# Zero-padded attention products: a second copy of the queries, last values laid out per head, 8 exp buffers for 12

## The chip, the cores and the metric

The kernel runs on one core of a Trainium2 chip. The metric is the device time of one launch in microseconds (us); lower is better. The engines are PE (matrix products; PEld is its loading of weights, that is of the operand that stays in the array), DVE and ACT (elementwise work), POOL (slower elementwise work) and SP, which here only issues DMAs.

## What is computed

```python
# attention: q, k, v are (4, 8, 576, 64)
q_rot, k_rot = (rotate(q), rotate(k))
scores = scale * np.matmul(q_rot, k_rot.transpose(0, 1, 3, 2))
scores = scores - np.max(scores, axis=-1, keepdims=True)
attn = np.exp(scores)
attn = attn / (np.sum(attn, axis=-1, keepdims=True) + 1e-09)
return np.matmul(attn, v)
# then, on the (2304, 512) result: a gated layer, (sigmoid(x Wg) * (x Wv)) Wo with d_ff 1536,
# and a layer of 8 experts, each token through one of them
```

The gated layer and the experts are not touched by the change.

## The kernel before

Attention works on 16 pairs of heads, one after the other. Products are made of two parts, a high and a low one, so that precision is kept: every matrix is split in a rounded high part and the rest.

A pair has nine score tiles (`scores`, line 164). Tile t = 2j + x below 8 is 128 queries of head x against the 576 keys, in two halves of 288 columns. It has two products. The first has 128 rows: high and low part of the queries stand one above the other in `q2`, and the high part of the keys stands twice in `kh`. The second has the high queries against the low keys `kl`; as a head has 64 dimensions, it has 64 rows, those of the head (`q2[r, x, qs]`, `kl[r]`). Tile 8 takes the last 64 queries of both heads; its third product uses `qd`, which holds the queries on a diagonal with zeros beside them, and so has 128 rows already.

DVE scales a tile out of PSUM into a buffer `e` (ring of E_BUFS), with the row's extreme (line 190); ACT takes the exponential (line 202). PE transposes it (line 234; the last 64 keys apart, line 249), ACT copies the high part out (`pth`, line 264; `p5h` for the last keys), DVE the low part (`ptl`, `p5l`, line 268). A value product (`value`, line 270) exists four times per pair, for head x and the query ranges 0 to 255 and 256 to 575: ten products into one PSUM buffer `pv`, eight of them with 128 rows for the first 512 keys, and two with 64 rows, `vv[r, 8]` against `p5h` and `p5l`, for the last 64 keys. ACT copies half of `pv`, DVE adds the other half to it.

The operands of a pair are prepared while earlier pairs run (`plan_prep`, from pair 2 on): a load from HBM, the rotation on POOL, the split, and then twelve copies by DMA from `hq` and `hk` into `q2`, `qd` and `kh` (line 448). These operands exist twice, for even and odd pairs: a pair's copies may begin when the score tiles of the pair two before are done, and its score tiles wait for all of them. The pairs 0 and 1 are prepared by the engines instead (`plan_direct`).

The order on each engine is set by a list scheduler (`Plan`): costs in us and priorities by tile decide which operation comes next; rings of buffers bound how far it goes ahead. SP, too, takes its DMAs in that order, each when the one before it has been issued.

Of the kernel before, what the change touches and what calls it, by code (L numbers as in the profile page):

```python
# [7 lines left out]
F32 = mybir.dt.float32  # L8
# [8 lines left out]
NP = H // 2  # L17
# [5 lines left out]
E_BUFS = 12  # L23
PT_BUFS = 3
ST_BUFS = 3
# [6 lines left out]
class Plan:  # L32
    """Orders instructions of several in-order engines: a list schedule over their dependences.
    Costs and latencies (us) only steer the order; the waits themselves are Tile's.
    A ring is a set of rotating buffers: an op that takes the next one has to stand behind the
    op that reads the old contents last."""
# [70 lines left out]
class Attention:  # L107
    def __init__(self, tc, pool, xpool, psum_s, psum_t, psum_v, qk, v, rope, ident, xt, rows):
        self.tc, self.nc = tc, tc.nc
        self.pool, self.xpool, self.ps_s, self.ps_t, self.ps_v = pool, xpool, psum_s, psum_t, psum_v  # L110
        self.qk, self.v, self.xt, self.rows = qk, v, xt, rows
        nc = self.nc
        self.rope = rope
        self.ident = ident
        t = lambda shape, dt, name: pool.tile(shape, dt, name=name, tag=name, bufs=1)
        self.pth = t([128, KC, 2 * S], F32R, "pth")
        self.ptl = t([128, KC, 2 * S], F32R, "ptl")
        self.p5h = t([128, S], F32R, "p5h")
        self.p5l = t([128, S], F32R, "p5l")
        self.vv = [t([128, 9, 2, D], F32R, f"vv_{i}") for i in range(2)]  # L120
        self.kl = [t([128, S], F32R, f"kl_{i}") for i in range(2)]
        self.qd = [t([128, 128], F32R, f"qd_{i}") for i in range(2)]
        sa = xpool.tile([128, 7 * S], F32R, name="sa", tag="sa", bufs=1)
        self.raw = f32(sa[:, 0:4 * S]).rearrange("p (a s) -> p a s", a=4)
        self.hqk = sa[:, 4 * S:7 * S].rearrange("p (a s) -> p a s", a=3)
        self.hq, self.hk = self.hqk[:, 0:2], self.hqk[:, 2]
        sb = xpool.tile([128, 4 * S + 4 * 640], F32R, name="sb", tag="sb", bufs=1)
        kh = sb[:, 0:4 * S].rearrange("p (i x s) -> p i x s", i=2, x=2)
        q2 = sb[:, 4 * S:].rearrange("p (i x s) -> p i x s", i=2, x=2)
        self.q2, self.kh = ([a[:, i] for i in range(2)] for a in (q2, kh))  # L130
        self.xv = t([128, 320], F32, "xv")
        self.vraw = t([128, 9, D], F32, "vraw")
        for i in range(2):
            nc.vector.memset(f32(self.q2[i][:, 0, S:640]), 0.0)
            nc.vector.memset(f32(self.q2[i][:, 1, 512:S]), 0.0)
            nc.vector.memset(f32(self.qd[i]), 0.0)
        self.e, self.s, self.pt, self.pv = {}, {}, {}, {}
        self.stat, self.ready, self.rt, self.rr = {}, {}, {}, {}
        self.plan = Plan(dict(s=2, e=E_BUFS, pt=PT_BUFS, pv=1))
        self.ids = {}  # L140

# [21 lines left out]
    def scores(self, T):  # L163
        """tile t of a pair: t = 2 j + x is queries 128 j.. of head x; t = 8 the last 64 of both heads"""
# [8 lines left out]
        else:  # L173
# [3 lines left out]
            mm = [(q2[:, x, qs], kh[:, x]), (q2[r, x, qs], kl[r])]  # L177
# [16 lines left out]
    def column(self, T):  # L194
        """statistics of a tile; columns of a head stand together"""
# [21 lines left out]
    def recip_rows(self, p, x, part):  # L217
        """the reciprocal sums of head x (its first 512 queries, or the rest) into each of its 64 partitions"""
# [25 lines left out]
    def transpose5(self, p, part):  # L244
        """the last 64 keys: head 1 in partitions 64.. (after 64 other keys), then head 0 in 0.."""
# [24 lines left out]
    def value(self, p, x, u):  # L270
# [4 lines left out]
        r = slice(64 * x, 64 * x + 64)  # L275
# [4 lines left out]
        mm += [(vv[r, 8], h[r, c0:c0 + w]) for h in (self.p5h, self.p5l)]  # L280
# [34 lines left out]
    def frees(self, last, first):  # L315
        """op last reads the buffer that op first took"""
# [39 lines left out]
    def plan_direct(self, p, pr):  # L356
        """the first pairs: rotation shared by two engines, operands doubled by the engines"""
# [6 lines left out]
        for half in (1, 0):  # L364
            j = 2 * half
            for n, c in enumerate(self.cuts(p, half)):
# [21 lines left out]
                for x in range(2):  # L388
                    last = min(c.stop, 512) if x else c.stop
                    cuts = [(c.start, last, 0)] + ([(512, S, 64)] if last < c.stop else [])  # L390
                    for a, b, d in cuts:
# [9 lines left out]
                        if a < 512:  # L401
                            for t in range(c.start // 128, 4):
                                need[x, t] = keys
# [8 lines left out]
    def plan_prep(self, p):  # L412
# [27 lines left out]
        for x in range(2):  # L440
            r = slice(64 * x, 64 * x + 64)
            cp.append((0, self.qd[i][r, r], self.hq[r, 0, 512:S]))
        for x in range(2):
# [23 lines left out]
    def plan_tile(self, T):  # L467
# [3 lines left out]
        self.op(("s", T), "PE", (0.74 if t == 8 else 0.5) * (1 if T > 4 else 2), lambda: self.scores(T), ready, T + o["s"], "s")  # L471
# [55 lines left out]
    def plan_value(self, p, x, u):  # L527
# [4 lines left out]
        self.op(("value", p, x, u), "PE", 10 * w / 2350, lambda: self.value(p, x, u),  # L532
# [34 lines left out]
def pack(q, k, v):  # L567
# [10 lines left out]
    vp = np.concatenate([vm, vp[:, :, :, 512:].reshape(B, NP, 128, 1, D)], axis=3)  # L578
# [22 lines left out]
class Gated:  # L601
    """x -> (sigmoid(x Wg) * (x Wv)) Wo, weights given as 64-bit words."""
# [16 lines left out]
    def convert(self, f, m, dma):  # L619
        """float64 words -> float32 (truncated) -> two float32r parts; returns (engine, cost, closure) in order."""  # L620
# [55 lines left out]
    def early_x(self, u):  # L676
        """parts of a unit's x in the memory that the last pair's rotation leaves"""
# [6 lines left out]
    def gate_val(self, f, u, keep=None):  # L684
        """keep: a free [128, 2, U] area for the result, instead of a pair of rotating tiles"""
# [12 lines left out]
    def gv_mm(self, f, m, p, xh, xl, chunks, part=None):  # L698
        """part 0: the products with the high part of x; 1: those with the low part; None: both, chunk by chunk"""
# [16 lines left out]
    def early(self, at, npairs):  # L716
        """the first units' part of the first matrix pair, in the engines' free time at the end of the attention;
        its results wait in the memory of later matrices"""
# [69 lines left out]
    def convert_group(self, grp):  # L788
        """closures; each matrix's load stands one matrix ahead of its arithmetic"""
# [8 lines left out]
    def opening(self):  # L798
        """the rest of the first group and the second; leaves the second's last unit to its out product"""
# [135 lines left out]
    def last(self, prev, r, experts):  # L935
        """The last group: all of its g first, with the router's logits from the y so far and from g;
        then its part of y, while the routing is worked out."""
# [37 lines left out]
        def before(u, prio):  # L975
            """the group before: its part of y"""
# [11 lines left out]
        def fold(prio):  # L988
            """the router's weights behind the last out matrices"""
# [125 lines left out]
def bc(ap, axis, n):  # L1115
    """insert a broadcast axis of size n"""
# [4 lines left out]
class Router:  # L1121
# [59 lines left out]
    def fold(self, k, c, parts, ps_pool):  # L1181
        """the router's weights behind an out matrix: wc = wo wg, split in two parts"""
# [46 lines left out]
    def route(self, plan, start, ps_pool, area):  # L1229
        """adds the routing of all tokens to the plan"""  # L1230
# [6 lines left out]
        def do(eng, cost, deps, fn, name=None):  # L1237
            """deps None: behind the one before"""
# [137 lines left out]
class Experts:  # L1376
# [10 lines left out]
    def keep_warm(self, n):  # L1387
        """products that nobody reads: the tensor engine's clock halves when it waits long"""
# [5 lines left out]
    def place(self):  # L1394
        """claims the memory in the order in which the part before frees it: what is written first last"""
# [11 lines left out]
    def load(self, s, k, dma=None):  # L1407
        """start loading part k of the weights of the expert of slot s"""
# [93 lines left out]
    def half1(self, s, h, x):  # L1502
        """first layer of half a slot: tokens in the output's partitions"""
# [27 lines left out]
    def half2(self, s, h, hx):  # L1531
        """second layer of half a slot"""
# [135 lines left out]
```

## Time and profile before

| | us |
|---|---|
| median of 3 runs | 1082.15 (1081.64 to 1085.84) |
| span of the profiled execution | 1086.7 |

The profiled execution shows its span alone, from its first to its last instruction; it is 4.5 us over the median of the runs, and over the slowest of them too. Attention takes about the first 365 us of the span; what follows is the gated layer and the experts. A busy PE in a profile is not PE at its peak: matmuls are pipelined, and what a matmul costs in a row of them is the distance between the starts of two, not the length shown for one.

### The profile page before, as it was taken

What the parts mean: (1) busy time and instruction counts of PE and PEld (TensorE: products, weight loads), DVE (VectorE), ACT (ScalarE), POOL (GpSimd) and SP (SyncE); (2) the same over time, 40 slices, a digit from 0 to 9 for tenths busy, and PEclk for the clock granted to TensorE, in tenths of its full rate; (3) what the DMA queues carried; (4) which work ended last, traced back from release to release, by engine and by line L of the source; (5) the groups of instructions that cost most, each with busy time, mean ns of one, the idle gap of its engine ahead of it and who ended that gap; (6) DMA issues with size and microseconds to landing.
All of it is one profiled execution on the core that took longest, in us unless ns stands there. A gap on an engine that the chain in (4) does not pass through costs nothing.

```text
span 1086.7 us, 16486 instructions
## 1 busy us (share of the span) xinstructions
PE 1044.1 (96%) x6035; PEld 916.1 (84%) x6035; DVE 663.1 (61%) x1175; ACT 531.9 (49%) x1051; POOL 380.2 (35%) x288
## 2 busy tenths in 40 slices
PE   4999999999999999999999999999998899999996
PEld 3778787877778899999999999999876699999995
DVE  6888887877777673653554444543247665555561
ACT  4877777877677742222222222223331555455552
POOL 4678657668430242322331322221142111121111
PEclk9999999999899999999999999999997999999998
DMA  5456565556421130210110111100015877776750
GB/s 183 133 160 174 140 179 145 142 153 157 121 69 58 42 117 21 60 40 20 59 59 20 59 40 40 39 1 1 1 49 183 284 238 223 243 224 221 222 177 23
DMA packets 71737, 122.78 MB, mean 113 GB/s; under 512 B 13967, under 2 KB 37151, under 8 KB 71648
## 3 DMA queue, kind: packets, MB, share of 16 engines
q1 hardware_dynamic: 57728, 104.07, 33.0%
q0 software_dynamic: 3040, 9.70, 2.7%
q10 hardware_dynamic: 10880, 7.87, 2.3%
q8 instruction: 50, 0.82, 0.3%
q14 instruction: 39, 0.32, 0.1%
HBM read 95.13 MB, written 9.77 MB: 97 GB/s over the span
## 4 chain that ended last, share of the span: by engine, by line
PE 72%; issue 15%; DMA 5%; DVE 4%; POOL 1%; ACT 1%; ACTq 0%; SPq 0%; POOLq 0%; DVEq 0%
PE gv L705 27%; PE yo L771 13%; PE s L180 10%; PE pv L282 10%; PE pt L234 6%; DMA out<-e_y,r_si 5%; PE pt L249 2%; POOL e_xg L1436 1%; PE s L705 1%; PE r_pl L1205 1%; PE r_pt L1169 1%; DMA rope<-in_rope 0%; POOL out L1499 0%; PE r_pl L1212 0%; DVE sb L396 0%
## 5 line engine op out<-in xcount | busy, mean ns | idle before, releaser
L714 POOL TENSOR_TENSOR gl<-sg,gh 128x384 fp32r<-128x384 f32 x60 | 64.2, 1069 | 258.6 <-ACT gh L713 258.6
L712 DVE TENSOR_TENSOR sg<-gv,sg 128x384 f32<-128x384 f32 x70 | 39.0, 557 | 141.5 <-PE gv L705 119.5
L190 DVE TENSOR_SCALAR_CACHE_REDUCE e<-s 128x576 f32<-128x576 f32 x144 | 107.1, 748 | 24.0 <-PE s L180 22.8
L202 ACT ACTIVATE e<-e,st 128x576 f32<-128x576 f32 x144 | 112.0, 780 | 5.6 <-DVE e L190 5.4
L1429 DVE TENSOR_TENSOR e_w<-wr,e_w 128x1024 fp32r<-128x1024 f32 x80 | 95.9, 1222 | 28.9 <-ACT e_w L1428 28.6
L711 ACT ACTIVATE sg<-gv 128x384 f32<-128x384 f32 x70 | 34.3, 490 | 140.4 <-PE gv L705 140.3
L268 DVE TENSOR_TENSOR ptl<-pt,pth 128x512 fp32r<-128x512 f32 x144 | 95.3, 683 | 10.6 <-ACT pth L264 9.5
L180 PE MATMUL s<-sb 128*128 128x288 f32 x320 | 81.1, 344 | 16.2 <-DVE sb L396 14.7
L264 ACT CAST pth<-pt 128x512 fp32r<-128x512 f32 x144 | 80.3, 587 | 30.2 <-PE pt L234 29.0
L1428 ACT CAST e_w<-wr 128x1024 fp32r<-128x1024 f32 x80 | 81.4, 1047 | 26.6 <-DMA x_rows<-xy 22.5
L1484 PE MATMUL e_py<-e_w,e_hh 128*128 128x512 f32 x288 | 89.7, 393 | 0.0
L159 POOL TENSOR_TENSOR sa<-sa,rope 128x1152 f32<-128x1152 f32 x28 | 74.5, 2663 | 32.2 <-DMA sa<-in_qk 27.3
L234 PE MATMUL pt<-cst,e 128*128 128x128 f32 x576 | 84.0, 285 | 1.6 <-DVE ptl L268 1.6
L1499 POOL DMA_INDIRECT out<-e_y,r_si x19 | 19.6, 1030 | 187.4 <-ACT e_y L1498 187.4
L1466 PE MATMUL e_ph<-e_xh,e_w 128*128 128x256 f32 x576 | 82.1, 286 | 0.7 <-ACT e_xh L1449 0.7
L713 ACT CAST gh<-sg 128x384 fp32r<-128x384 f32 x60 | 30.8, 514 | 101.1 <-DVE sg L712 101.0
L282 PE MATMUL pv<-pth,vv 128*128 128x256 f32 (+1 forms) x256 | 75.8, 318 | 3.6 <-DVE vv L347 2.2
L705 PE MATMUL gv<-xe,wb 128*128 128x384 f32 x384 | 78.9, 338 | 0.0
L1466 PEld LDWEIGHTS e_ph<-e_xh,e_w 128*128 128x128 f32 x576 | 75.9, 195 | 1.5 <-ACT e_xh L1449 0.9
L234 PEld LDWEIGHTS pt<-cst,e 128*128 128x128 f32 x576 | 64.7, 144 | 13.6 <-issue 8.2
L705 PE MATMUL gv<-xh,wb 128*128 128x384 f32 x288 | 74.1, 338 | 0.0
L180 PEld LDWEIGHTS s<-sb 128*128 128x128 f32 x320 | 49.3, 196 | 27.8 <-DVE sb L396 14.7
(242 smaller groups left out, 2496.1 us busy)
## 6 DMA issues: line engine op xcount, KB each, us to landing
wr<-in_w SPq DMA_DIRECT2D x74, 512.0 KB, 4.1
sa<-in_qk SPq DMA_DIRECT2D x30, 576.0 KB, 4.7
sb<-sa SPq DMA_DIRECT2D x84, 144.0 KB, 4.9
wraw<-in_wg SPq DMA_DIRECT2D x12, 512.0 KB, 3.9
wraw<-in_wv SPq DMA_DIRECT2D x12, 512.0 KB, 3.5
wraw<-in_wo SPq DMA_DIRECT2D x12, 512.0 KB, 3.6
vraw<-in_v SPq DMA_DIRECT2D x16, 288.0 KB, 5.2
x_rows<-xy ACTq DMA_DIRECT2D x18, 256.0 KB, 2.6
```

Of the source, the lines that this page charges most:

```text
L180: nc.tensor.matmul(ps[:, u, 0:SH], a, m[:, SH * u:SH * u + SH], start=n == 0, stop=n == len(mm) - 1)
L190: self.nc.vector.tensor_scalar(out=e, in0=ps[:, :, 0:SH], scalar1=-0.125, scalar2=3.0e38, op0=ALU.mult, op1=ALU.min, accum_out=st[:, 0])
L202: nc.scalar.activation(out=e, in_=e, func=AF.Exp, bias=st[:, 0], scale=-1.0, accum_out=st[:, 1])
L234: nc.tensor.transpose(pt[:, c], e[:, 128 * c:128 * c + 128], self.ident)
L268: self.nc.vector.tensor_tensor(out=lo, in0=src, in1=f32(hi), op=ALU.subtract)
L282: nc.tensor.matmul(ps[:, 0:w], a, m, start=n == 0, stop=n == len(mm) - 1)
L705: self.nc.tensor.matmul(p[:, 0:U], a[:, wc], b[:, c], start=c == 0 and n == 0, stop=c == KC - 1 and n == 2)
L771: nc.tensor.matmul(ps, a, b, start=n == 0, stop=n == 3 * len(GROUPS[grp]) - 1)
L1428: nc.scalar.copy(out=hi, in_=raw)
L1429: nc.vector.tensor_tensor(out=lo, in0=raw, in1=f32(hi), op=ALU.subtract)
L1466: nc.tensor.matmul(ps[:, k], a[:, fs], b[:, c], start=n == 0, stop=n == 3 * KC - 1)
L1484: nc.tensor.matmul(ps, a[:, f, hs], b, start=n == 0, stop=n == 23)
```

## The change

The second product of a score tile gets 128 rows in all pairs but the first. Its queries come from a new tile `qz`, which holds the high queries of head x in that head's 64 rows and zeros in the other 64, and it takes all rows of `kl`. The two products with the last 64 keys get 128 rows as well: the values of the last keys are stored once per head, with zeros in the rows of the other head. `qz` is filled by two more DMAs per pair; the loads of the values grow from 576 to 640 columns. The ring of `e` has 8 buffers for 12, that of the row statistics 2 for 3. The scheduler's costs of score tiles and value products change, so the order on the engines moves. (The diff also removes docstrings, which are left out here.)

```diff
-E_BUFS = 12
+E_BUFS = 8
 PT_BUFS = 3
-ST_BUFS = 3
+ST_BUFS = 2
...
-        self.vv = [t([128, 9, 2, D], F32R, f"vv_{i}") for i in range(2)]
+        self.vv = [t([128, 10, 2, D], F32R, f"vv_{i}") for i in range(2)]
...
+        self.qz = [t([128, 2, 512], F32R, f"qz_{i}") for i in range(2)]
...
+            for x in range(2):
+                nc.vector.memset(f32(self.qz[i][64 - 64 * x:128 - 64 * x, x]), 0.0)
...
-            mm = [(q2[:, x, qs], kh[:, x]), (q2[r, x, qs], kl[r])]
+            mm = [(q2[:, x, qs], kh[:, x]), (q2[r, x, qs], kl[r]) if p == 0 else (self.qz[i][:, x, qs], kl)]
...
-        mm += [(vv[r, 8], h[r, c0:c0 + w]) for h in (self.p5h, self.p5l)]
+        mm += [(vv[:, 8 + x], h[:, c0:c0 + w]) for h in (self.p5h, self.p5l)]
...
+                            if p > 0:
+                                self.dma(("qz", *key), 0.4, lambda x=x, i=slice(a, min(b, 512)): nc.sync.dma_start(
+                                    out=f32(self.qz[p][r[x], x, i]), in_=f32(q2[r[x], x, i])), [("qhi", *key)], pr + 1.5 + x + n)
...
             cp.append((0, self.qd[i][r, r], self.hq[r, 0, 512:S]))
+            cp.append((0, self.qz[i][r, x], self.hq[r, 0, 0:512]))
...
-        self.op(("s", T), "PE", (0.74 if t == 8 else 0.5) * (1 if T > 4 else 2), lambda: self.scores(T), ready, T + o["s"], "s")
+        self.op(("s", T), "PE", (0.81 if t == 8 else 0.54 if p else 0.92) * (1 if T > 4 else 2), lambda: self.scores(T), ready, T + o["s"], "s")
...
-        self.op(("value", p, x, u), "PE", 10 * w / 2350, lambda: self.value(p, x, u),
+        self.op(("value", p, x, u), "PE", 10 * (w / 2400 + 0.0135), lambda: self.value(p, x, u),
...
-    vp = np.concatenate([vm, vp[:, :, :, 512:].reshape(B, NP, 128, 1, D)], axis=3)
+    ve = np.zeros((B, NP, 2, 64, 2, D), v.dtype)
+    for x in range(2):
+        ve[:, :, x, :, x] = vp[:, :, x, 512:]
+    vp = np.concatenate([vm, ve.reshape(B, NP, 128, 2, D)], axis=3)
```

Two places show how instructions move. The first is PE behind tile 8 of pair 8 (`s<-kl_0,qd_0` is that tile's last product; the score tiles behind it are those of pair 9, `pt` are transposes). Before:

```order
L180 MATMUL s_2214<-kl_0_99,qd_0_101 128x288 x2
L180 MATMUL s_2225<-sb_104 128x288 x2
L180 MATMUL s_2225<-kl_1_100,sb_104 128x288 x2
L234 MATMUL pt_2234<-cst_60,e_2103 128x128 x4
L234 MATMUL pt_2242<-cst_60,e_2113 128x128 x4
L180 MATMUL s_2251<-sb_104 128x288 x2
L180 MATMUL s_2251<-kl_1_100,sb_104 128x288 x2
L234 MATMUL pt_2259<-cst_60,e_2137 128x128 x4
L180 MATMUL s_2267<-sb_104 128x288 x2
L180 MATMUL s_2267<-kl_1_100,sb_104 128x288 x2
```

Of the change:

```order
L183 MATMUL s_2251<-kl_0_99,qd_0_101 128x288 x2
L237 MATMUL pt_2262<-cst_60,e_2067 128x128 x4
L183 MATMUL s_2271<-sb_106 128x288 x2
L183 MATMUL s_2271<-kl_1_100,qz_1_104 128x288 x2
L237 MATMUL pt_2279<-cst_60,e_2145 128x128 x4
L183 MATMUL s_2288<-sb_106 128x288 x2
L183 MATMUL s_2288<-kl_1_100,qz_1_104 128x288 x2
L237 MATMUL pt_2297<-cst_60,e_2190 128x128 x4
L183 MATMUL s_2304<-sb_106 128x288 x2
L183 MATMUL s_2304<-kl_1_100,qz_1_104 128x288 x2
```

The second product of a tile reads `qz` in place of `q2` (which lies in `sb`), and one transpose stands between two score tiles. No instruction is added on PE.

The second place is SP, from the first copy of pair 9 to its last (`sa<-in_qk` are loads of later queries and keys, `vraw` one of values; `sb<-sa`, `qd` and `qz` are the copies). Before:

```order
L448 DMA sb_104<-sa_103 64x576 x2
L326 DMA sa_103<-in_qk 128x1152
L448 DMA sb_104<-sa_103 64x576 x2
L448 DMA sb_104<-sa_103 64x512
L448 DMA sb_104<-sa_103 64x64
L448 DMA sb_104<-sa_103 64x512
L448 DMA sb_104<-sa_103 64x64
L448 DMA qd_1_102<-sa_103 64x64 x2
L448 DMA sb_104<-sa_103 64x576 x2
```

Of the change:

```order
L455 DMA sb_106<-sa_105 64x576 x2
L328 DMA sa_105<-in_qk 128x1152
L455 DMA sb_106<-sa_105 64x576 x2
L455 DMA sb_106<-sa_105 64x512
L455 DMA sb_106<-sa_105 64x64
L455 DMA sb_106<-sa_105 64x512
L455 DMA sb_106<-sa_105 64x64
L455 DMA qd_1_102<-sa_105 64x64
L455 DMA qz_1_104<-sa_105 64x512
L455 DMA qd_1_102<-sa_105 64x64
L455 DMA qz_1_104<-sa_105 64x512
L338 DMA vraw_108<-in_v 128x640
L455 DMA sb_106<-sa_105 64x576 x2
```

Twelve copies and one load have become fourteen copies and two loads.

## Rows read from the trace of the kernel before

**Rows 1.** The page: span, busy time, and the chain that ended last.
```profile
span 1086.7 us, 16486 instructions
PE 1044.1 (96%) x6035; PEld 916.1 (84%) x6035; DVE 663.1 (61%) x1175; ACT 531.9 (49%) x1051; POOL 380.2 (35%) x288
...
PE 72%; issue 15%; DMA 5%; DVE 4%; POOL 1%; ACT 1%; ACTq 0%; SPq 0%; POOLq 0%; DVEq 0%
```
**Rows 2.** Busy us (instructions) per engine by stage, granted clock, DMA share, GB/s.
```profile
28.00:65.00 37.00, 33.20 (x207) 26.12 (x207) 31.21 (x66) 30.26 (x70) 26.77 (x17) 1.00 0.53 146
...
110.00:280.00 170.00, 169.43 (x1058) 135.06 (x1057) 136.41 (x310) 132.56 (x313) 114.23 (x69) 1.00 0.61 157
```
**Rows 3.** Products with `qd` (two per pair): durations, first and last start.
```profile
L180 PE MATMUL s<-kl,qd x32: 291/295/302, 30.9 to 334.3; 128*128 128x288 f32 x32
```
**Rows 4.** Who waited for whom from 100 to 350 us: total, times, longest.
```profile
POOL sa L159 <- DMA sa<-in_qk: 20.5, 11, 5.6
PEld s L180 <- issue: 20.0, 120, 0.3
POOL kl L431 <- PE s L180: 17.8, 5, 6.5
DVE e L190 <- PE s L180: 15.2, 17, 1.7
```
**Rows 5.** Timeline of PE and PEld, two score tiles, then a value product of 256 columns.
```profile
200.25 0.50 PE L180 MATMUL s<-sb 128*128 128x288 f32 x2
...
200.68 0.29 PEld L180 LDWEIGHTS s<-kl,sb 64*128 64x128 f32 x2 [0.16 <-issue]
...
202.06 0.39 PE L282 MATMUL pv<-pth,vv 128*128 128x256 f32 x1
...
202.40 0.19 PEld L282 LDWEIGHTS pv<-ptl,vv 128*128 128x128 f32 x1
...
202.52 0.28 PE L282 MATMUL pv<-ptl,vv 128*128 128x256 f32 x1
...
202.99 0.28 PE L282 MATMUL pv<-ptl,vv 128*128 128x256 f32 x1
...
203.63 0.88 PE L249 MATMUL pt<-cst,e 128*128 128x128 f32 x6
```
**Rows 6.** Timeline of PE: tile 8 of pair 9, and what follows.
```profile
213.30 0.43 PE L180 MATMUL s<-kl,qd 128*128 128x288 f32 x2
213.57 0.60 PE L234 MATMUL pt<-cst,e 128*128 128x128 f32 x4
```
**Rows 7.** Timeline of PE: a value product of 320 columns, first to last, and what follows.
```profile
277.46 0.41 PE L282 MATMUL pv<-pth,vv 128*128 128x320 f32 x1
...
278.00 0.31 PE L282 MATMUL pv<-ptl,vv 128*128 128x320 f32 x1
...
278.58 0.31 PE L282 MATMUL pv<-ptl,vv 128*128 128x320 f32 x1
...
279.30 0.87 PE L249 MATMUL pt<-cst,e 128*128 128x128 f32 x6
```
**Rows 8.** Timeline of SP: first and last copies of pair 11, then its first tile on PE.
```profile
215.75 1.12 SPq L448 DMA_DIRECT2D sb<-sa  x2
...
223.83 2.52 SPq L448 DMA_DIRECT2D sb<-sa  x4
...
233.49 0.43 PE L180 MATMUL s<-sb 128*128 128x288 f32 x2
```
**Rows 9.** Copies issued from 220 to 250 us: issue, and time to landing.
```profile
L448 SPq DMA_DIRECT2D sb<-sa x17: 461/588/2634, 219.6 to 245.9; - x17
...
DMA to landing us min/median/max: 2.5/4.1/5.3
```
**Rows 10.** Timeline of DVE: the memsets, the first load's use, two later instructions.
```profile
1.21 0.11 DVE L135 MEMSET sb<- 128x64 f32 x1
1.30 0.17 DVE L136 MEMSET qd<- 128x128 f32 x1
5.78 0.46 DVE L161 TENSOR_TENSOR sa<-sa,rope 128x288 f32<-128x288 f32 x1 [4.31 <-DMA rope<-in_rope]
...
205.20 0.73 DVE L190 TENSOR_SCALAR_CACHE_REDUCE e<-s 128x576 f32<-128x576 f32 x1
...
205.87 0.67 DVE L268 TENSOR_TENSOR ptl<-pt,pth 128x512 fp32r<-128x512 f32 x1
```
**Rows 11.** Two stretches around a wait of PE, columns as in the second group.
```profile
282.00:284.30 2.30, 0.93 (x7) 0.56 (x6) 2.24 (x3) 1.46 (x3) 2.22 (x2) 0.99 0.01 2
284.30:291.10 6.80, 6.80 (x27) 5.80 (x27) 4.01 (x9) 2.38 (x5) 1.98 (x2) 0.50 0.16 47
```

More of the change, by code (lines that the diff above doesn't have):

```diff
@@ L131, in __init__ @@
         self.xv = t([128, 320], F32, "xv")
-        self.vraw = t([128, 9, D], F32, "vraw")
+        self.vraw = t([128, 10, D], F32, "vraw")
         for i in range(2):
@@ L274, in value @@
         cs = slice(S * x + c0, S * x + c0 + w)
-        r = slice(64 * x, 64 * x + 64)
         ps = self.ps_v.tile([128, 512], F32, name="pv", tag="pv")
@@ L401, in plan_direct @@
                         if a < 512:
+                            if p > 0:
+                                self.dma(("qz", *key), 0.4, lambda x=x, i=slice(a, min(b, 512)): nc.sync.dma_start(
+                                    out=f32(self.qz[p][r[x], x, i]), in_=f32(q2[r[x], x, i])), [("qhi", *key)], pr + 1.5 + x + n)
+                                keys = keys + [("qz", *key)]
                             for t in range(c.start // 128, 4):
```

## The prediction

> **What bounds the kernel now.** First the page: PE is busy for 96% of the span and makes 72% of the chain that ended last, and a further 15% of that chain is "issue", time in which an engine waited for nothing that the profile shows [rows 1]. Next the windows by stage. From 110 to 280 us, in attention, PE is busy for 169.4 of 170 us, DVE for 136.4, ACT for 132.6, POOL for 114.2 [rows 2]. The two `qd` products, which run once per pair, go from 30.9 to 334.3 us: 303.4 over 15 pairs, so 20.2 us per pair [rows 3]. A pair thus uses 16.2 us of DVE (136.4 / 170 x 20.2), 15.8 of ACT, 13.6 of POOL, and all of PE. The waits agree: DVE waits for PE's scores, while PE's weight loads for scores wait 120 times, 20.0 us in total, for "issue" [rows 4].
>
> What that issue time is shows in the timeline. Two score tiles begin at 200.25 and are over at 202.06, where a value product begins: 0.905 us for a tile's four products of 288 columns. Between them the weight load of the 64-row product stands idle for 0.16 us and then begins together with its matmul [rows 5]. Inside the value product, with 128 rows throughout, a weight load of 0.19 us begins at 202.40, its matmul at 202.52, and the matmul before it still runs: starts are 0.12 us apart (202.52 to 202.99 is four of them) [rows 5]. So a product is cheap next to others with 128 rows, and dear where 64 rows begin, go on or end.
>
> **Prices with 128 rows throughout.** For 288 columns, the `qd` products already have 128 rows: two in 0.27 us (213.30 to 213.57), 0.135 each [rows 6]. For 256 columns 0.118 [rows 5]. For 320, four in 0.58 us (278.00 to 278.58), 0.145 each [rows 7].
>
> **What it removes on PE.** A score tile: 4 x 0.135 = 0.54 instead of 0.905, 0.365 less, eight times per pair: 2.9 us. A value product of 256 columns takes 1.57 us now (202.06 to 203.63) [rows 5], and ten at 0.118 make 1.18; one of 320 takes 1.84 (277.46 to 279.30) [rows 7], and ten at 0.145 make 1.45. That is 0.39 each, four per pair: 1.6 us. In all 4.5 us of 20.2, which leaves PE at 15.7 per pair. Pair 0 keeps its 64-row score products. Columns are not added, and the number of products is the same. That zeros cost nothing beyond the rows they fill is taken from `qd`, half of which is zeros.
>
> A rule of the Trainium skill speaks against this. Its page "TensorE: Matmul & The Clock Gate", Part 3 (Packing small matmuls), says that a weight load overlaps with running matmuls only when its row group differs, and its section "Why this matters for your kernels" says that a product with few rows takes as long as a full one, so that small ones should be kept in separate rows. By that, padding would save nothing here and the time would stay at 1082. The loads at 202.40 overlap within one row group [rows 5], so on this point the trace disagrees.
>
> **What it adds.** Two copies of 128 KB per pair on SP; a copy's issue takes 0.59 us (median) [rows 9], so 1.2 us per pair. Four memsets of 512 columns on DVE: 64 columns take 0.11 us and 128 take 0.17 [rows 10], so some 0.5 us each, 2.1 in all, beside the 4.31 us for which DVE waits for its first load [rows 10]: nothing; without that cover 2 us. Wider value tiles (640 columns for 576) on ACT or POOL: a ninth of one operation of each, under 0.2 us per pair, on engines that have room. The smaller rings: with 8 buffers DVE can take three tiles of the next pair before the last transposes of this one (line 249) have read theirs, with 12 seven. The trace shows no wait of that kind; I take zero, and half a microsecond per pair as the upper end.
>
> **What is late next.** PE at 15.7 is not alone any more: DVE needs up to 16.2 us. Instructions on DVE overlap a little (one of 0.73 us begins at 205.20, the next at 205.87) [rows 10]; with some 37 per pair (310 / 170 x 20.2) at 0.06 this makes 14 to 16.2. And there is the chain of the copies. Pair 9's last tile is done at 213.57 [rows 6]; only then may pair 11's operands be written (POOL's wait of 17.8 us for PE, at line 431, is this one [rows 4]); the first copy is issued at 215.75, the last of the last four ends its issue at 226.35, so was issued at 225.8 [rows 8], and lands 2.5 to 4.1 us later [rows 9], at 228.3 to 229.9. Pair 11 starts on PE at 233.49 [rows 8], so this chain now has 3.6 to 5.2 us to spare. With 1.2 us more it has 2.4 to 4.0 us, and a period of 20.2 can shrink by no more than that: to 16.2 to 17.8 us.
>
> So three limits lie between 15 and 18 us, where one stood alone at 20.2. The nearest rows for such a state are those from 28 to 65 us, where PE is not the only bound: PE busy for 33.2 of 37 us, 90% [rows 2]. 15.7 / 0.9 would be 17.4; the middle of the copies' limits is 17.0. I take 17.2, 3.0 us less per pair.
>
> **The sum.** The two pairs behind pair 0 are paced by their preparation (those same 37 us), and I give them 2 us together; 13 pairs at 3.0 make 39. That is 41 us. The profiled span of 1086.7 goes to 1045.7; the runs, whose median lies 4.5 us lower, go to 1041. The ends: 0 if padding saves nothing, 13 x 4.5 + 2 = 60 if PE keeps pace alone. One loss is in the 20.2 already: from 282.0 to 284.3 PE is busy for 0.93 of 2.3 us, and in the 6.8 us behind it the granted clock is 0.50, the lower of its two levels (1.2 GHz of 2.4) [rows 11], which costs 3.4 us. I count one such event in the changed kernel as well.
>
> **The rivals.**
> - PE stays the bound: copies begin earlier, DVE's overlap is full, and a pair takes 15.7 to 16.3 us. For it: DVE at 80% and POOL at 67% leave room [rows 2]. Against it: the copies' chain. Gain 13 x 4.2 + 2 = 57, time 1025; chance 0.15.
> - The other engines keep more of it: DVE and ACT in order, each behind the other, with two or three PSUM buffers between them, and PE's clock falls more often, as PE now idles in places. A pair takes 18 to 19.5 us. Gain 13 x 1.5 + 2 = 21, time 1061; chance 0.17.
> - Padding does not do what it says: a 128-row load behind a 128-row score product is as slow as now. Against it: `qd` [rows 6]. Time 1082; chance 0.03. The page of the Trainium skill named above, in the two sections named, would come out here.
> - It ends slower: the copies become the bound at more than 20.2 us per pair. The queue of SP carries them in order behind loads; one issue in [rows 9] took 2.63 us instead of 0.59. It decides when the two new copies, with what they hold up, lengthen the chain by over 5.2 us instead of 1.2. At 6.2 a pair takes 21.2 us: 13 x 1.0 = 13 us more, 1095. For it: DMA is busy for 61% already [rows 2]. Against it: the other issues are far shorter, and the median landing is 4.1 us. Chance 0.04.
>
> **How the numbers follow.** The forecast, 16.4 to 18 us per pair (1029 to 1052), has 0.61; its middle is 1041. For 8 in 10, the range takes in most of the first rival's cases and two thirds of the second's: 1020 to 1065. About 0.5% (5.4 us) is what a measurement of this kernel can tell from no change. Faster by more than that: 0.61 + 0.15 + 0.16 = 0.92. Within it: 0.01 of the second rival and most of the third, 0.04. Slower: 0.04.
>
> **What the changed profile would show.** Score products of 288 columns start 0.135 us apart, and "issue" disappears from the waits of PE's loads; if it stays there, the removal is wrong. The `qd` products come every 17.2 us. PE shows waits within attention where it had almost none, for DVE or for the copies; if for the copies mostly, the chain above is the bound; if for none, the first rival holds. The stages behind attention take as long as before; if they move by several us, the sum misses a term. The forecast fails most easily in the 17.2, which is a choice between limits and not a row.

## The result, and the profile of the changed kernel

The changed kernel takes 1059.22 us (median of 4 runs, 1056.3 to 1062.35), the kernel before 1083.88 (4 runs, 1081.64 to 1085.84): a ratio of 0.9768, with a 95% interval of 0.9741 to 0.9794. That is 24.7 us less, where 41 was forecast. The time stands where the second rival put it (1061). Both profiled executions are the longest of their four runs, 3.1 us over the median for the changed kernel and 2.0 for the kernel before. The page of the changed kernel: span, busy time, and the chain that ended last.

```profile
span 1060.5 us, 16517 instructions
PE 994.1 (94%) x6035; PEld 912.6 (86%) x6035; DVE 664.0 (63%) x1179; ACT 532.9 (50%) x1051; POOL 386.3 (36%) x288
...
PE 52%; issue 17%; DMA 12%; DVE 9%; ACT 4%; POOL 3%; SPq 2%; ACTq 0%; POOLq 0%; DVEq 0%
```

PE's share of the chain fell from 72% [rows 1] to 52%, and DMA, 5% of it before, has 12%. The windows (columns as in [rows 2]):

```profile
28.00:65.00 37.00, 33.82 (x220) 30.95 (x220) 34.95 (x74) 29.46 (x70) 28.98 (x19) 0.95 0.65 182
...
110.00:265.00 155.00, 137.16 (x1007) 128.48 (x1007) 128.09 (x293) 127.96 (x298) 109.96 (x67) 0.98 0.69 178
```

In attention PE was busy for 99.7% of the time [rows 2]; now for 137.16 of 155 us, 88%. No engine is full: DVE and ACT are busy for 83%. The `qd` products answer to [rows 3]:

```profile
L183 PE MATMUL s<-kl,qd x32: 291/295/442, 35.6 to 312.3; 128*128 128x288 f32 x32
```

They span 276.7 us, 18.4 us per pair, where it was 20.2. So the 26.2 us that the span lost (1086.7 to 1060.5) have three parts: pair 0 ends 4.7 us later (35.6 for 30.9), the 15 pairs behind it take 26.7 us less (276.7 for 303.4), and what follows the last `qd` product takes 4.2 us less (748.2 for 752.4).

On PE the products became cheaper, as the change intended. The timeline of PE: a score tile behind a transpose, a value product of 256 columns, and a score tile that follows tile 8:

```profile
200.32 0.60 PE L252 MATMUL pt<-cst,e 128*128 128x128 f32 x4
200.69 0.53 PE L183 MATMUL s<-sb 128*128 128x288 f32 x2
201.05 0.42 PE L183 MATMUL s<-kl,qz 128*128 128x288 f32 x2
201.31 0.28 PE L284 MATMUL pv<-pth,vv 128*128 128x256 f32 x1
...
202.50 0.60 PE L237 MATMUL pt<-cst,e 128*128 128x128 f32 x4
...
203.74 0.42 PE L183 MATMUL s<-sb 128*128 128x288 f32 x2
...
204.26 0.60 PE L237 MATMUL pt<-cst,e 128*128 128x128 f32 x4
```

A score tile takes 0.52 us (203.74 to 204.26), or 0.62 behind a transpose (200.69 to 201.31); it was 0.905 [rows 5]. The value product takes 1.19 us (201.31 to 202.50), and was 1.57; behind a transpose such a product takes longer, one of 320 columns 1.54 (299.96 to 301.50) for 1.47 behind a score tile (173.41 to 174.88). By busy time PE uses 16.3 us per pair (137.16 / 155 x 18.4), by the prediction's prices 15.7. Who waits now is in the waits from 65 to 280 us, total, times, longest:

```profile
POOL sa L162 <- DMA sa<-in_qk: 37.5, 16, 4.8
DVE xy L301 <- ACT xv L292: 17.4, 14, 3.8
PEld s L183 <- DVE e L193: 15.3, 24, 2.0
ACT sa L152 <- POOL sa L160: 10.0, 5, 3.2
PE s L183 <- DVE e L193: 8.2, 11, 1.7
...
PEld s L183 <- issue: 5.8, 4, 2.3
ACT sa L152 <- DMA sb<-sa: 5.5, 3, 2.2
...
ACT sa L152 <- issue: 3.6, 1, 3.6
...
ACT sa L152 <- DMA recip_rows<-rt: 2.9, 1, 2.9
```

The "issue" waits of PE's loads, 120 in [rows 4], are four here (three in the stretch of that group, 100 to 350 us). The rest reads as a chain: POOL waits for the loads of later queries and keys; ACT, in order, stands at their split (L152, 22.0 us in these four rows); behind it stand the copies of value products (L292), for which DVE waits; and PE waits for DVE's evacuation of scores. Whether that chain sets the pace is what the runs are for. In the chain that ended last, from 134 to 173 us (start, us, what; pieces are left out at the dots), it closes into a loop:

```profile
134.24 8.77 DMA sa<-in_qk
...
145.95 3.51 DMA sb<-sa
...
149.60 0.69 POOL sa L154
...
153.55 0.68 DVE sa L437
...
154.25 7.61 DMA sa<-in_qk
...
164.94 3.49 DMA sb<-sa
...
168.60 0.12 ACT sa L152
...
170.53 0.57 ACT sa L152
...
171.11 0.43 ACT xv L292
...
171.98 0.76 DVE e L193 x2
...
172.78 0.80 PE s L183 x4
```

A load is issued at 134.24; the last copy that SP issues behind it lands at 149.46; then the next half is split (high part at 149.60, here on POOL, low part at 153.55), and with that done the next load is issued, 20 us after the first. It lands after 7.61 us, and only then does SP issue the last five copies behind it (L455). The last of them lands at 168.43; ACT may then split the next half (L152) and, further on, copy a value product (L292); DVE evacuates scores; PE begins a tile. SP's timeline in that stretch shows copies that wait for a load that they don't read:

```profile
154.25 0.48 SPq L328 DMA_DIRECT2D sa<-in_qk  x1
154.76 4.88 SPq L455 DMA_DIRECT2D sb<-sa  x6
159.74 0.54 SPq L455 DMA_DIRECT2D qd<-sa  x1
161.87 0.46 SPq L455 DMA_DIRECT2D qz<-sa  x1
```

SP issues seven copies behind the load (154.76 to 160.28) and stands until the load has landed, before the eighth. Whether the program's own waits or the queue make it stand there, no run shows.

### The profile page after: what moved, and what is told of

Same layout as the page of the kernel before. It is cut to its first block, busy times and chain, and to the rows that moved or that the text cites. A ratio compares the mean times of both kernels' runs of the same rounds, so it can differ in the third digit from the quotient of the medians.

```text
span 1060.5 us, 16517 instructions
## 1 busy us (share of the span) xinstructions
PE 994.1 (94%) x6035; PEld 912.6 (86%) x6035; DVE 664.0 (63%) x1179; ACT 532.9 (50%) x1051; POOL 386.3 (36%) x288
## 4 chain that ended last, share of the span: by engine, by line
PE 52%; issue 17%; DMA 12%; DVE 9%; ACT 4%; POOL 3%; SPq 2%; ACTq 0%; POOLq 0%; DVEq 0%
PE gv L715 28%; PE yo L781 13%; DMA out<-e_y,r_si 5%; DMA sa<-in_qk 4%; PE pv L284 3%; DMA sb<-sa 3%; PE s L183 3%; DVE e L193 2%; SPq L455 2%; PE pt L237 2%; DVE ptl L271 1%; ACT e L205 1%; POOL e_xg L1446 1%; ACT pth L267 1%; PE s L715 1%
## 5 line engine op out<-in xcount | busy, mean ns | idle before, releaser
L724 POOL TENSOR_TENSOR gl<-sg,gh 128x384 fp32r<-128x384 f32 x60 | 64.2, 1070 | 263.3 <-ACT gh L723 263.3
L183 PE MATMUL s<-sb 128*128 128x288 f32 x320 | 78.1, 335 | 33.5 <-DVE sb L398 14.0
L1438 ACT CAST e_w<-wr 128x1024 fp32r<-128x1024 f32 x80 | 81.4, 1047 | 23.9 <-DMA x_rows<-xy 19.8
L1509 POOL DMA_INDIRECT out<-e_y,r_si x19 | 19.6, 1030 | 187.2 <-ACT e_y L1508 187.2
L237 PEld LDWEIGHTS pt<-cst,e 128*128 128x128 f32 x576 | 68.7, 144 | 8.8 <-DVE ptl L271 4.5
```

Of the source, the lines that this page charges most:

```text
L183: nc.tensor.matmul(ps[:, u, 0:SH], a, m[:, SH * u:SH * u + SH], start=n == 0, stop=n == len(mm) - 1)
L237: nc.tensor.transpose(pt[:, c], e[:, 128 * c:128 * c + 128], self.ident)
```

## The experiments

The theory, L in the expectations: the preparation of a pair's operands (load, rotation, split, copies, with one raw buffer and one queue on SP) now sets the pace. Its rivals, as they came up: the two `qz` copies' traffic; ACT's splits, in order ahead of PE's helpers; SP's queue; the order on the engines as such (theory E: DVE, ACT and PE, in order and with few buffers, need 18.4 us for a pair by themselves, and the preparation only follows); and PE, which may still pay for every microsecond. Dots in an edit stand for lines left out.

**The halves.** Values padded alone, with the small rings, in the kernel before:

```diff
-E_BUFS = 12
+E_BUFS = 8
...
-ST_BUFS = 3
+ST_BUFS = 2
...
-        mm += [(vv[r, 8], h[r, c0:c0 + w]) for h in (self.p5h, self.p5l)]
+        mm += [(vv[:, 8 + x], h[:, c0:c0 + w]) for h in (self.p5h, self.p5l)]
...
```

> The kernel before with the padded values and the smaller rings, but with the 64-row score products, without qz: the value half of the change alone. The prediction's term: four value products at 0.39 us each less, 1.6 us per pair, 24 us in all, 1060, as no copy is added and PE still is the bound at 18.6 us per pair. Theory L agrees, as its loop has 3 us to spare there. If a 64-row product costs only where it meets a 128-row one, and the value product's saving is smaller: 1070.

Measured: 1069.06 us, ratio 0.9884 (0.9865 to 0.9904), 9 us short of the gain that the prediction's term gives. Its `qd` products:

```profile
L180 PE MATMUL s<-kl,qd x32: 291/295/302, 31.2 to 319.1; 128*128 128x288 f32 x32
```

That is 19.2 us per pair. A value product of 256 columns takes 1.29 us there behind a 64-row score product (200.04 to 201.33) and 1.27 behind a transpose (203.44 to 204.71), where it took 1.57 and 1.56 (33.02 to 34.58): some 0.28 less, not 0.39. Four make 1.1 us per pair, which puts PE at 19.1, and PE is busy for 152.58 of 155 us (110 to 265 us). So PE still sets the pace there and the whole of a smaller price comes through, which gives the time of the expectation's last case (1070). The score half alone, in the changed kernel:

```diff
-        mm += [(vv[:, 8 + x], h[:, c0:c0 + w]) for h in (self.p5h, self.p5l)]
+        mm += [(vv[r, 8], h[r, c0:c0 + w]) for h in (self.p5h, self.p5l)]
...
```

> The score half of the change alone: qz and its copies, rings of 8 and 2, but the values of the last keys stored once and their two products with 64 rows, as before. PE then needs 20.2 - 2.9 = 17.3 us per pair, more than the 15.5 of the whole change, and still less than the 18.43 that a pair of the changed kernel takes. Theory L (the preparation of the operands paces the changed kernel's pairs, not PE): a pair still takes about 18.4 us, the last qd products stand near 312 us and the time stays within 5 us of the change, about 1060; value padding is then worth 13 us only where it is made alone. Theory P (every us less on PE still shortens a pair in part): the 1.6 us that PE has more per pair come back for the most part, a pair takes 19.2 to 19.8 us, last qd products near 325 to 332, time 1072 to 1080. A time of 1065 to 1072 would mean that both share it.

Measured: 1068.89 us, 0.9868 (0.9845 to 0.9892), the case in which both theories share.

```profile
L183 PE MATMUL s<-kl,qd x32: 291/295/311, 35.9 to 318.7; 128*128 128x288 f32 x32
```

18.85 us per pair, 1.5 over PE's price of 17.3. With the whole change it is 18.4, 2.7 over 15.7. The lower PE's price, the less of it comes through: of the last 1.1 to 1.6 us, 0.4. If that is PE's doing, the preparation is no sharp floor; but the planner's costs differ between the two, and so does the order on the engines. The rings alone, in the kernel before:

```diff
-E_BUFS = 12
+E_BUFS = 8
...
-ST_BUFS = 3
+ST_BUFS = 2
```

> The kernel before with 8 exp buffers for 12 and 2 statistics buffers for 3, nothing else. Theory L and the prediction: no wait on these rings, 1083 as before, within 3 us. Theory R (the smaller ring holds back DVE behind the last transposes of a pair, and part of the missing gain is this): slower by 5 to 15 us.

Measured: 1089.42 us, 1.0042 (1.001 to 1.0074): 4.6 us slower by the ratio, more than the 3 us allowed for no effect, and just short of the 5 that theory R gives at least. Its `qd` products span 305.7 us (32.5 to 338.2) instead of 303.4.

**Where the 18.4 comes from.** The loads of pairs 2 to 15 bring 64 of their 576 columns, and the rest of the buffer keeps older numbers; every instruction stays where it was.

```diff
             h = slice(2 * half, 2 * half + 2)
+            cols = cols if p < 2 else slice(0, 64)
```

> The changed kernel, with the loads of queries and keys of pairs 2 to 15 cut from 576 to 64 columns, so that most of these operands are stale; order and number of DMAs stay. Theory L: a load lands in some 3 us instead of 7 to 9, and SP does not stop for it any more; 4 us less in the loop of each pair, so that DVE becomes the bound at 16.2 to 16.8 us per pair: 1030. Theory E: 1059, at most 3 us less.

Measured: 1045.88 us, 0.9645 (0.9612 to 0.9678).

```profile
L183 PE MATMUL s<-kl,qd x32: 291/295/442, 39.8 to 296.4; 128*128 128x288 f32 x32
```

17.1 us per pair, 1.3 less, with no other edit. Pair 0 ends 4.2 us later than in the changed kernel (39.8 for 35.6), so of the 20.1 us that the pairs behind it win 16.1 are left in the span (1060.5 to 1044.4). Its waits from 65 to 280 us:

```profile
DVE xy L301 <- ACT xv L292: 8.7, 13, 1.2
POOL sa L162 <- DMA sa<-in_qk: 7.5, 7, 2.7
...
PE s L183 <- DVE e L193: 5.3, 12, 1.2
...
ACT sa L152 <- POOL sa L160: 2.2, 2, 1.5
```

Every link of the chain shrinks with the first: 37.5 to 7.5, 10.0 to 2.2, 17.4 to 8.7, 8.2 to 5.3. SP's wait of its copies for loads, 18.8 us (13 times) in the changed kernel, is gone too. The cut frees bandwidth as well as time to landing; the run doesn't part the two. The same cut in the kernel before is the control.

> The kernel before, with the loads of queries and keys of pairs 2 to 15 cut from 576 to 64 columns (most of these operands are stale): the control to the small loads of the changed kernel, which took 13 us off. If PE alone set the pace of the kernel before and the loads were hidden behind it, nothing: 1082, within 4 us. If loads slow things by sharing the memory or the engines whatever the bound is: 1070.

Measured: 1091.41 us, 1.0068 (1.0045 to 1.0092).

```profile
L180 PE MATMUL s<-kl,qd x32: 291/295/302, 30.4 to 337.4; 128*128 128x288 f32 x32
```

There is no gain over the whole, though POOL's wait for loads falls from 23.9 to 0.6 us (65 to 280 us). The distances of the last `qd` products of neighbouring pairs, in us, worked out from the starts in each trace:

```
before                       21.3 23.7 17.2 20.8 19.8 19.9 19.9 19.5 20.3 19.9 17.9 17.0 27.3 19.8 19.0
before, values padded alone  26.2 19.9 21.1 16.0 18.4 18.8 21.6 18.8 16.5 18.7 18.1 18.8 18.4 18.7 17.9
before, small loads          30.3 22.9 17.2 20.8 19.8 19.9 19.9 19.5 20.3 19.9 17.9 17.0 22.7 19.8 19.0
the change                   15.9 19.5 16.2 20.8 22.3 16.7 18.3 20.9 17.0 18.3 20.6 14.8 19.2 19.9 15.8
the change, small loads      17.7 17.2 16.6 19.7 17.8 16.7 16.8 19.6 14.7 17.0 15.7 14.7 19.2 17.1 15.9
```

The kernel before and its copy with small loads agree to 0.1 us in twelve of fifteen places. The copy wins 0.8 us in the second distance and 4.6 in the thirteenth, which holds the wait of [rows 11]; behind the first distance that makes 5.4 us, where the same cut wins 21.6 us in the changed kernel. So before the change the loads were hidden in all but two places. The loss stands in the first distance (pair 1): PE waits there 3.19 us for DVE, until 38.87, and then the granted clock is at its lower level:

```profile
38.00:52.00 14.00, 13.13 (x47) 10.11 (x47) 7.71 (x19) 4.47 (x11) 5.32 (x5) 0.51 0.10 24
```

**The new copies.** One column instead of 512 in each `qz` copy of these pairs, the order unchanged (the memsets of `qz` take all 128 rows, so that the rest is zero):

```diff
...
-            cp.append((0, self.qz[i][r, x], self.hq[r, 0, 0:512]))
+            cp.append((0, self.qz[i][r, x, 0:1], self.hq[r, 0, 0:1]))
```

> The changed kernel, with each qz copy of pairs 2 to 15 cut from 512 columns to one, so that the second score product of these pairs reads other queries; order on all engines and the number of DMAs stay. Theory L (the pairs are paced by a closed loop of the preparation: load of queries and keys, rotation, split, copies by DMA on SP's queue, next split, next load; PE, DVE and ACT wait for it): 256 KB per pair less beside the loads, which take 7 to 9 us to land when they meet the copies; a pair goes from 18.4 to about 17.7 us, the time to 1049. If only the issue slots of the two DMAs matter in that loop: 1058. Theory E (DVE, ACT and PE, in order and with few buffers, need 18.4 us for a pair by themselves, and the preparation only follows): 1059.

Measured: 1059.87 us, 0.9766 (0.9732 to 0.98). The same as the change: their bytes cost nothing, and theory L's 1049 did not come. Without the copies for pairs 2 to 15, so that their score products read a `qz` of zeros or old queries:

```diff
...
-            cp.append((0, self.qz[i][r, x], self.hq[r, 0, 0:512]))
```

> The changed kernel without the two qz copies of pairs 2 to 15, so that their second score product reads zeros or old queries; the scheduler places 20 DMAs per pair on SP instead of 22, and the order shifts a little. Theory L: the loop loses two issues (1.2 us) and their traffic; a pair goes from 18.4 to about 17 us, the time to 1038 to 1042, which is the prediction's sum without its two added copies. Theory E: 1059.

Measured: 1066.4 us, 0.9846 (0.9808 to 0.9884): 7 us over the change, with two DMAs less per pair. The planner orders the engines anew once they are gone, and in this order POOL waits for loads for 47.5 us (65 to 280 us) instead of 37.5. So the copies' price can't be read from a run without them. The copies made by POOL, and by ACT, instead of DMA:

```diff
-            cp.append((0, self.qz[i][r, x], self.hq[r, 0, 0:512]))
...
+            self.op(("qz", p, x), "POOL", 0.65, lambda r=r, x=x: self.copy("POOL", self.qz[i][r, x], f32(self.hq[r, 0, 0:512])),
...
```

> The changed kernel, with qz written by POOL from the split queries (rows of a head stay in their rows) instead of by DMA: two operations of 0.7 us on POOL per pair, nothing left out. Theory L: the loop loses two issues and the traffic, but POOL, which carries rotation and splits in that loop, has 1.4 us more; a pair at 17.5 to 18 us, 1046 to 1053. Theory E: 1059.

Measured: 1058.59 us, 0.9779 (0.9763 to 0.9796), no different from the change, with two DMAs less per pair on SP. POOL waits for loads for 16.0 us there (65 to 280 us) instead of 37.5, and a pair still takes 18.2 us (36.2 to 309.8): the length of that wait alone does not tell the pace.

> The changed kernel, with qz written by ACT from the split queries instead of by DMA: two operations of 0.5 us on ACT per pair, nothing left out. Theory L: the loop loses two issues and the traffic; ACT goes from 15.2 to 16.2 us of work per pair: a pair at 17 to 17.7 us, 1040 to 1050. Theory E (ACT is part of what paces a pair): 1065, slower than the change by 6 us.

Measured: 1068.61 us, 0.9873 (0.9854 to 0.9892), slower than the change. PE's value products wait for DVE (L301) for 13.8 us, where it was 2.7: that fits a busier ACT that delays what DVE needs of it. Here too the order is new.

**Links of the loop.** All splits on POOL, so that ACT stands at none:

```diff
...
+    HI = dict.fromkeys(((p, h) for p in range(2, 16) for h in range(2)), "POOL")
```

> The changed kernel, with the high part of queries and keys split off by POOL in all pairs, where ACT did 19 of 28. In the changed kernel ACT waits 16 us of 155 at these splits for rotation, copies or loads, and behind them stand its copies for the value products, for which DVE waits 12.6 us and then PE for DVE; before, ACT never waited there. Theory A (this standing in line on ACT is how late preparation reaches PE): ACT's waits at the split vanish, a pair goes from 18.4 to 17.5 us or less, the time to 1046 or less. Theory L (the loop itself is too long, whoever does the split): the loop gets no shorter, as POOL has 0.9 us more per pair; 1059 or more.

Measured: 1068.67 us, 0.9846 (0.9805 to 0.9888). In its waits (65 to 280 us) ACT's splits are gone, and PE waits for the copies themselves:

```profile
POOL sa L162 <- DMA sa<-in_qk: 23.6, 13, 4.4
...
PE s L183 <- DMA sb<-sa: 9.1, 3, 4.0
...
PE s L183 <- DMA qz<-sa: 3.6, 3, 1.7
```

To take ACT's standing away is thus not enough. Why the time is worse is not parted: the split takes longer on POOL (0.69 us at 149.60, for 0.57 on ACT at 170.53), the order is new, and the granted clock is 0.94 from 110 to 265 us, where it was 0.98. Loads issued by POOL instead of SP:

```diff
...
-                self.dma(("load", p, half, n), size, ld(half, cols), [("lo", p - 1, half)], at)
...
+                    self.op((("load", p, half, n), "issue"), "POOL", 1.0, ld(half, cols, nc.gpsimd), [("lo", p - 1, half)], at)
...
```

> The changed kernel, with the loads of queries and keys of pairs 2 to 15 issued by POOL instead of SP, nothing left out. On SP a copy some eight DMAs behind a load stands until the load has landed, about 2 us per pair. Theory Q (this stop on SP's queue is a large part of the loop): a pair 1 us shorter, 1045 to 1050. Against it: POOL pays some 1 us for each issue, and is part of the loop: 1059 or more.

Measured: 1067.01 us, 0.9838 (0.9798 to 0.9877), slower than the change; POOL waits for loads for 28.6 us instead of 37.5, and a pair takes 18.7 us (35.3 to 316.2). SP's queue alone does not explain the 18.4 either, though POOL pays for the issues here (0.59 us each) and the order is new.

Taken together: theory L forecast a gain of 6 to 21 us for each of four edits on the copies, and none came (1059.87 for 1049, 1066.4 for 1038 to 1042, 1058.59 for 1046 to 1053, 1068.61 for 1040 to 1050). Theory E's 1059 holds for two of these, but small loads would have won 3 us at most by it, and won 13. They did not reach theory L's 1030 either: at 17.1 us per pair PE is busy for 95% of the time from 110 to 265 us, DVE and ACT for 90%. So the loads are shown to hold 1.3 of the 2.7 us that a pair takes over PE's price of 15.7 (2.1 over its busy time); for the rest, engines in order of which none is full, no run names a cause.

**Pair 0.** In the changed kernel the four steps of a conversion of later weights (L652 to L666) stand on DVE between the first score evacuations, as its timeline shows:

```profile
17.05 0.75 DVE L193 TENSOR_SCALAR_CACHE_REDUCE e<-s 128x576 f32<-128x576 f32 x1
...
17.84 1.28 DVE L652 TENSOR_SCALAR wt<-wt 128x512 f32<-128x512 f32 x1
19.15 0.43 DVE L657 TENSOR_SCALAR wt<-wt 128x512 int32<-128x512 int32 x1
19.50 0.75 DVE L193 TENSOR_SCALAR_CACHE_REDUCE e<-s 128x576 f32<-128x576 f32 x1
```

and PE waits there for DVE, five times from 17.9 to 30 us, 3.3 us in total (once, 0.5 us, in the kernel before); one of them:

```profile
20.31 0.85 PE L183 MATMUL s<-sb 128*128 128x288 f32 x2 [0.82 <-DVE e L193]
```

The clock comes in as well. Of pair 0's score products with 64 rows, one in the kernel before and one in the changed kernel:

```profile
28.46 0.53 PE L180 MATMUL s<-kl,sb 64*128 64x288 f32 x2
...
32.98 0.85 PE L183 MATMUL s<-kl,sb 64*128 64x288 f32 x2
```

The longer length is that of the stretch at a granted clock of 0.50 in [rows 11] (0.85 us at 287.76), so PE was at the lower level until 33 us at least here, and until some 28 before. The clock column has 1.00 for both stretches; this rests on the lengths. Conversions were put behind the pair's last evacuation:

```diff
-                dep = [("khi", 0, 1, 1, 1), ("cv", n - 2, 5)]
+                dep = [("khi", 0, 1, 1, 1), ("tsa", 8), ("cv", n - 2, 5)]
```

> The changed kernel, with the weight conversions that fill free time held back until DVE has taken the last score tile of pair 0. In the changed kernel four of them stand on DVE between the first score tiles, PE waits there for DVE and its clock rises 8 us later than before; the last qd product of pair 0 comes 4.7 us later than before. Theory F (these conversions are the cause): that product is back at 31 us, and the time falls by 4 to 5 us, to 1055, if nothing later takes it back. Against it: the conversions come later and stand in the way of other pairs, whose DVE is fuller now than PE: 1059.

Measured: 1066.21 us, 0.984 (0.9804 to 0.9876). The theory fell: pair 0 ends at 34.5 instead of 35.6, 1.1 of the 4.7 us, and the time is worse. What the runs do say is which half brings the delay: the first `qd` product stands at 31.2 with values padded alone and at 32.5 with the rings alone, but at 35.9 with scores padded alone. The edits of that half that reach pair 0 are the copies of pair 1's `qz`, its memsets, and the planner's costs of score tiles; which of them it is was not tried.

## Why the prediction came out as it did

The time lies inside the stated range (1020 to 1065), which took in two thirds of the second rival's cases, and outside the forecast proper (1029 to 1052; by its own sum the lower end is 1082 - 13 x 3.8 - 2 = 1031). That the range held owes more to the rival than to the forecast's mechanism.

- **What padding removes on PE: right, if priced a little high.** A score tile was priced at 0.54 us and takes 0.52, or 0.62 behind a transpose; a value product of 256 columns at 1.18 and takes 1.19 behind a score tile. The value half alone saves some 0.28 us per value product and not 0.39. "Issue" all but went from PE's loads, as said. A page of the Trainium skill, "TensorE: Matmul & The Clock Gate", Part 3, says that a weight load overlaps with running products only where its row group differs. That does not hold here: the ten products from 201.31 to 202.50, all with 128 rows and a new weight load each, stand 0.119 us apart.
- **What the change adds: right for the copies, within its range for the rings.** The copies were priced at 1.2 us of SP per pair, within the slack; with one column each the time is the same, and so it is with their issues gone from SP (copies by POOL). The rings were priced at nothing to half a microsecond per pair; alone they cost 0.42% (0.1% to 0.74%), the loss standing in the first three distances (71.3 us for 62.2), where the granted clock is 0.51 from 64.5 to 75 us. So they were not free, as the sum had it, and what is theirs and what the clock's is not parted.
- **The 17.2 us per pair: the step that failed.** It is the term of the sum that was mis-sized, and measured 18.45 (276.7 / 15; 18.2 in the runs with one column and with the copies by POOL). The prediction set the copies' limit from the last tile of pair 9 to the landing of pair 11's copies, and chose a middle of 16.2 to 17.8. That chain begins too late: the copies need split data, the split needs a rotation, and the rotation a load into the one raw buffer. POOL's wait for these loads, 20.5 us in 11 times, is the first row of [rows 4]; of POOL's two rows there the prediction used the other one only. Before, that wait cost next to nothing (small loads there: equal distances in twelve of fifteen places); after, cutting the loads brings 18.4 to 17.1 us, near what was forecast without a loads' term. That agreement is in the size; which part of the cut does it (the landing, the bandwidth, SP's standing) is open. Over 15 pairs, with the 41 us spread as the sum had it, 262.4 us were expected from first to last `qd` product and 276.7 came: 14.3 us.
- **The clock: under-sized.** One fall was counted. In attention there are four, of 3.4 us at a granted clock of 0.50 each, two of them here:

```profile
115.00:118.40 3.40, 3.40 (x16) 3.40 (x16) 2.66 (x8) 2.86 (x8) 1.70 (x2) 0.50 0.81 215
231.10:234.50 3.40, 3.40 (x15) 3.36 (x14) 1.85 (x4) 1.87 (x6) 1.93 (x1) 0.50 1.02 284
```

  An estimate by half speed makes them cost at most 4 x 1.7 = 6.8 us against 3.4 before: 3.4 of the 14.3 us. It does not come on top of the loads' part: with small loads the records show no fall in attention, where PE idles less.
- **Pair 0 and the end: terms that were missing.** Pair 0 ends 4.7 us later, which no step foresaw; it goes with the score half, with PE's waits for DVE and a clock that is later at its upper level. Behind the last `qd` product 4.2 us were won where nothing was forecast: the gated layer's first products come 1.4 us sooner after it, near the 1.6 us that four value products were to save, and 2.8 us lie behind that layer's last such products, where the change touches nothing. There the granted clock is 0.51 for 13.8 us before (823.4 to 837.2) and for 7.0 us now (801 to 808), at most 3.4 us by half speed, which would cover them. These 2.8 us would then be no merit of the padding. 14.3 + 4.7 - 4.2 = 14.8 us, which is 41 less the 26.2 of the span.
- **The rivals.** The second rival had the time right and half the mechanism: DVE and ACT in order behind each other, and a clock that falls more often, are both seen. The loads, which it does not name, are shown to hold half or more of what a pair takes over PE's need. PE as the only bound (15.7 to 16.3 us) is out with PE idle for 12%; padding without effect is out by the prices; copies over 20.2 us did not come.

Open: what holds the rest, 17.1 us with small loads against PE's 15.7 to 16.3; and why orders with less work (no `qz` copies, conversions moved) are slower by 7 us. The order is fixed before the run, from planned times in which a load has 1.64 us and 1.0 more to landing (`plan_loads`, `LAT`), while a load lands in 4.7 us in the median in the kernel before (65 to 290 us) and in up to 8.77 us in the changed one. That this is why one order fits and another doesn't is only argued; other planned times were not tried on the chip.

## What to carry to other kernels

When a bound is taken away, the next limit can be a closed loop of preparation, so follow each operand back to its load and through every single buffer; a large wait of an engine that is off the path now (POOL for loads, first row of the waits) is a candidate, but only that. To test it, shrink that transfer in both kernels: no gain before and a gain after shows that it counts, and the size of the gain shows for how much. In a kernel with an order fixed ahead, an experiment that removes or moves an operation also deals a new order; without the `qz` copies the time was 7 us worse, so change sizes in place and leave the instructions where they stand.

## What the hardware showed that was not expected

- Mixing products of 64 and 128 rows cost 0.3 to 0.4 us per group: four products of 288 columns take 0.905 us mixed and 0.52 to 0.62 with 128 rows throughout; two 64-row products at the end of ten cost 0.28 us (1.57 to 1.29 with values padded alone), and 0.38 where the score product ahead has 128 rows too (1.19). The Trainium skill's page "TensorEngine Tiling (Array Packing)", "Key Properties", says that changing the tiling mode drains the engine; if a product on half of the rows counts as such a change, the traces agree.
- A load of 576 KB took up to 8.77 us to land beside the copies, and SP's issue of a later, unrelated copy, the eighth copy behind the load in the stretch shown, stood behind it, 18.8 us in 13 times from 65 to 280 us (12.8 us in 9 times in the kernel before). Whether this is the chip's doing or the program's is not shown.
- Smaller loads in the kernel before, a cut that takes nothing from PE, made pair 1 longer by 9 us (30.3 for 21.3). PE had waited 3.19 us for DVE, and the granted clock was 0.51 from 38 to 52 us, where the kernel before has 1.00. One fall of the clock can hide a gain of several us.
